# Attention feeding a swish MLP on one core: batches 0 and 1 piece by piece, and norms moved into early pass 2

## The chip, the cores and the metric

The kernel runs on one core of a Trainium2 chip. The metric is device time in microseconds (us), the median of several executions. A profile records one execution; its span is about 2 us shorter than the time of that execution (362.9 against 364.7 for the kernel before).

The engines are PE (matmuls and transposes; "PEld" is its weight load), DVE, ACT (exp, silu, copies), POOL, and SP, which issues DMAs. ACT and POOL can issue DMAs too. In the traces below each engine takes its own instructions in the order in which they were written: at 155.59 in the kernel before, a norm whose data had long been ready starts only when the evacuation written before it is done.

## The reference

```python
q_s = softmax(q, axis=-1)                 # over head_dim, 64
k_s = softmax(k, axis=2)                  # over the sequence, 576
kv  = einsum('bhsd,bhse->bhde', k_s, v)
out = einsum('bhsd,bhde->bhse', q_s, kv)  # batch 8, heads 8, seq 576, head_dim 64
x   = out.transpose(0, 2, 1, 3).reshape(4608, 512)
h   = x @ w_in                            # w_in 512 x 2048
g   = h / (1 + exp(-beta * h))
y   = g @ w_out                           # w_out 2048 x 512
```

## The kernel before

The 4,608 tokens form nine slabs: slabs 0 to 7 hold the first 512 tokens of batches 0 to 7, slab 8 the remaining 64 tokens of every batch. A slab has two passes of 64 matmuls of 128x512: pass 1 multiplies by w_in and applies silu (result in `GT`), pass 2 multiplies by w_out for four units `u` of 128 tokens, each of which is then evacuated: copied from PE's accumulators (`PS`) to `O2S`, from where it is stored. Attention of batch t+1 is spread as small steps between the matmuls of slab t; a counter of matmuls, the slot, says when a step is issued. Heads go in pairs, `hp` 0 to 3.

Attention of a batch consists of: exp of q and k (ACT), the norm of q (DVE: sum, reciprocal, multiply; `EQ`), the cast of v to bf16 (POOL; `VB` and the remainder `VR`), transposes of q (PE) and their copy to `QT`, the kv matmuls (PE), their masked and scaled copy `KVD` (DVE), the output matmul (PE), and the copy to `XT`, the input of pass 1.

```python
def norm_main(b, hp0, n):                      # three DVE instructions; a = EQ of n head pairs
    add(DVE, lambda e: e.tensor_reduce(s_, a, AX.X, ALU.add), ...)
    add(DVE, lambda e: e.reciprocal(v_, s_), ...)
    add(DVE, lambda e: e.tensor_tensor(a, a, vb, ALU.mult), ...)
def norm(b):
    norm_main(b, 0, 4)
    if b % 2 == 1:
        norm_rem()
# ... head: loads
add(ACTE, ... dma_start(BT, beta) ...)         # 8 KB, first on ACT's queue
load_main("qf", qt_h, QF, 0, split=4)          # SP
load_rem("krf", kt_h, KRF, 0, eng=ACTE)
load_main("kf", kt_h, KF, 0, eng=ACTE, split=4)
load_rem("vrf", vt_h, VRF, 0)
load_main("vf", vt_h, VF, 0, split=4)
gate = P.ops[-2]                               # the third of V's four loads
for c in range(8):                             # w_in, issued by POOL, cast to bf16 by the DMA
    add(POOL, lambda e, c=c, a=a: e.dma_start(WIN[:, :, 256 * c:256 * c + 256], a),
        ..., after=[gate] if c == 0 else ())
# ... head: batch 0
for hp in range(NHP):
    exp_main("q", QF, EQ, 0, hp, 1)
    norm_main(0, hp, 1)
exp_rem("k", KRF, EKR[0], ("ekr", 0))
cast_vr(0)                                     # POOL, behind the eight w_in issues
for hp in range(NHP):
    exp_main("k", KF, EK, 0, hp, 1)
    cast_v(0, hp)                              # POOL
    for s in t_steps(0, (hp,), HEAD) + kv_steps(0, (hp,), HEAD):
        s()
    if hp < 3:
        warm(3, 0)                             # matmuls on zeros
    for s in out_step(0, hp, HEAD, ACTE if hp % 2 else DVE):
        s()
# ... the slabs
for t in range(NSLAB):
    steps = attn(t + 1) if t < 7 else []
    lo, hi = {0: (90, 128), 1: (84, 128)}.get(t, (4, 112))   # slots of the steps
    ...                                        # pass 1; in slab 0 also the scaling of w_out
    if t == 0:
        prep(1)                                # exps and V casts
        norm(1)
    elif t == 1:
        prep(2)
        norm(2)
    for us in (((0, 1), (2, 3)) if t == 0 else ((0,), (1,), (2,), (3,))):
        pass2_group(t, us, tick)               # matmuls, then the evacuation to O2S (DVE)
        ...                                    # prep(3), or prep(t + 2) after unit 0
    if t == 1:
        norm(3)
    elif t >= 2 and t + 2 < B:
        norm(t + 2)                            # behind the last evacuation of the slab
    store(t)
```

The softmax here doesn't subtract the row's maximum and nothing guards it: scores larger than these inputs give would overflow.

## Time and profile before

| | before |
|---|---|
| median time | 366.3 us |
| span of the profile | 362.9 us |
| mean granted PE clock | 0.914 of full |
| PE busy | 299.7 us (83%) |

The first view is the profile's table of forty equal slices, 9.07 us each. A digit is the busy share in tenths; PEclk is the granted clock in tenths of full speed.

```profile
PE   5047973999569499959995999599959999999995
...
PEclk9559995799969899989999899889987999999999
```

From slice 14 on, the dips in the PE row come every four slices, at the starts of slabs 2 to 6; the earlier ones lie in the head and in pass 2 of slabs 0 and 1. PEclk dips with them or just after. The second view lists what PE waited for: total us, number of times, longest.

```profile
PE PS L340 <- DVE EQ L289: 38.0, 8, 7.2
PE PS L342 <- POOL VB L304: 13.9, 1, 13.9
```

The 38 us are waits of the transposes for the multiply of the norm. Of the eight waits one is in the head (2.9 us), one in slab 0 (6.7), one in slab 1 (7.2), and one at the start of each of slabs 2 to 6 (4.2 to 4.5 each). The 13.9 us is the head's wait for the first V cast, which stands on POOL behind the issues of w_in. In the lines of a timeline the columns are start, duration, engine (with a q where it only issues a DMA), line, operation, operands, count, and in brackets the idle time before it with its releaser:

```profile
14.65 6.16 POOL L473 DMA_DIRECT2D WIN<-in_moe_w_in_dram  x8 [9.27 <-DMA VF<-in_v_dram]
...
22.34 2.78 POOL L304 CAST VB<-VF 128x512 bf16<-128x512 f32 x4
```

The third view is the timeline at the start of slab 3, reduced to DVE and PE.

```profile
154.78 1.67 PE L342 MATMUL PS<-XT,WIN 128*128 128x512 bf16 x7
...
154.98 0.69 DVE L538 COPY O2S<-PS 128x512 f32<-128x512 f32 x1 [2.16 <-PE PS L342]
155.59 2.27 DVE L287 TENSOR_REDUCE QS<-EQ 128x32 f32<-128x2048 bf16 x1
...
158.28 2.29 DVE L289 TENSOR_TENSOR EQ<-EQ,QI 128x2048 bf16<-128x2048 bf16 x1
...
160.63 0.23 PE L340 MATMUL PS<-IDB,EQ 128*128 128x128 bf16 x1 [4.18 <-DVE EQ L289]
```

The norm's data were ready long before, but its instructions stand behind the last evacuation (154.98). PE does seven matmuls of the new slab, meets the first transpose, and waits.

The fourth view gives the busy time and clock by stage, with the stages cut at the first w_in matmul of a slab: the head, slab 0, slab 1, slab 2, slabs 3 to 6, slabs 7 and 8. Columns: stretch, its length, busy us and instructions of PE, PEld, DVE, ACT and POOL, the granted clock, the DMA share and GB/s.

```profile
0.00:32.60 32.60, 12.44 (x64) 6.15 (x66) 12.20 (x34) 6.77 (x11) 13.82 (x31) 0.74 1.00 209
32.60:77.10 44.50, 35.73 (x179) 16.47 (x181) 20.57 (x39) 20.19 (x29) 8.06 (x10) 0.85 0.99 303
77.10:116.90 39.80, 32.40 (x168) 15.30 (x170) 12.87 (x21) 23.02 (x36) 6.12 (x10) 0.91 0.66 200
116.90:154.80 37.90, 32.86 (x179) 15.68 (x181) 17.08 (x29) 18.35 (x27) 2.46 (x4) 0.95 0.40 126
154.80:303.70 148.90, 131.11 (x684) 63.07 (x697) 58.00 (x94) 66.06 (x97) 8.14 (x10) 0.93 0.16 54
303.70:362.90 59.20, 55.12 (x252) 24.92 (x255) 6.23 (x9) 22.01 (x32) 0.00 (x0) 0.99 0.15 54
```

In the last stage nothing but the passes is left, and 256 matmuls take 59.2 us with the tail; slab 7 alone takes 27.6. An estimate for a slab with attention is about 31 us: these 27.6 and some 3 us of attention matmuls (25 us for eight batches, by the sum in the prediction). A slab that takes longer is waiting or running at a lower clock.

### The profile page before, as it was taken

How to read it: one execution, taken by the hardware profiler on the slowest of the kernel's cores; microseconds unless marked ns; L12 is line 12 of the kernel's file. 1: busy time of each engine (PE TensorE's matmuls, PEld its weight loads, DVE VectorE, ACT ScalarE, POOL GpSimd, SP SyncE). 2: the span in 40 equal slices, each digit the busy share in tenths (PEclk: the TensorE clock that was granted, in tenths of full speed). 3: DMA queues.
4: the chain of work that ended last, by engine and by line, in shares of the span. 5: the costliest groups of instructions: out<-in, count | busy, mean ns of one | idle time of the engine just before them, and what ended most of it. 6: DMA issues, size and time to landing. Idle time of an engine off the chain costs nothing.

```text
span 362.9 us, 3757 instructions
## 1 busy us (share of the span) xinstructions
PE 299.7 (83%) x1514; PEld 141.6 (39%) x1544; DVE 127.0 (35%) x225; ACT 156.4 (43%) x232; POOL 38.6 (11%) x65
## 2 busy tenths in 40 slices
PE   5047973999569499959995999599959999999995
PEld 2023431544234155424442454244424544444442
DVE  3424418350255811560257125601571252011011
ACT  4105882038940178216822583158405603803710
POOL 4360004420004002030110020000000000000000
PEclk9559995799969899989999899889987999999999
DMA  8899899880399300960095000200020002002013
GB/s 225 212 162 264 315 316 337 235 274 36 121 313 337 127 2 11 342 169 0 5 321 167 0 2 0 116 3 0 3 116 0 0 2 116 2 0 116 2 29 87
DMA packets 45954, 44.29 MB, mean 122 GB/s; under 512 B 13665, under 2 KB 42353, under 8 KB 44913
## 3 DMA queue, kind: packets, MB, share of 16 engines
q1 hardware_dynamic: 39216, 40.11, 35.1%
q0 software_dynamic: 4224, 2.10, 4.6%
q10 hardware_dynamic: 2496, 1.84, 1.8%
q8 instruction: 12, 0.20, 0.2%
q14 instruction: 6, 0.04, 0.0%
HBM read 36.71 MB, written 9.44 MB: 127 GB/s over the span
## 4 chain that ended last, share of the span: by engine, by line
PE 68%; DVE 14%; DMA 11%; ACT 2%; SPq 2%; issue 1%; POOL 1%
PE PS L342 65%; DVE EQ L289 4%; DVE QS L287 4%; DMA QF<-in_q_dram 3%; PE PS L340 3%; DMA WIN<-in_moe_w_in_dram 3%; DMA VF<-in_v_dram 2%; DMA WST<-in_moe_w_out_dram 2%; DVE XT L406 1%; DVE O2S L538 1%; ACT EQ L273 1%; POOL WIN L473 1%; SPq L247 1%; DVE QI L288 1%; DVE KVD L390 1%
## 5 line engine op out<-in xcount | busy, mean ns | idle before, releaser
L533 ACT ACTIVATE GT<-PS,BETA 128x512 bf16<-128x512 f32 x144 | 98.8, 687 | 159.1 <-PE PS L342 158.8
L342 PE MATMUL PS<-WOUT,GT 128*128 128x512 bf16 x560 | 142.9, 388 | 2.0 <-DVE O2S L538 1.4
L342 PE MATMUL PS<-XT,WIN 128*128 128x512 bf16 x563 | 142.2, 397 | 1.1 <-DVE XT L406 0.4
L342 PEld LDWEIGHTS PS<-WOUT,GT 128*128 128x128 bf16 x576 | 52.8, 99 | 58.7 <-issue 3.6
L342 PEld LDWEIGHTS PS<-XT,WIN 128*128 128x128 bf16 x576 | 53.1, 102 | 57.5 <-issue 6.5
L340 PE MATMUL PS<-IDB,EQ 128*128 128x128 bf16 x128 | 29.4, 252 | 38.3 <-DVE EQ L289 38.0
L538 DVE COPY O2S<-PS 128x512 f32<-128x512 f32 x36 | 24.6, 688 | 75.6 <-PE PS L342 75.5
L342 PE MATMUL PS<-VB,EK 128*128 128x129 bf16 x128 | 26.2, 226 | 15.0 <-POOL VB L304 13.9
L340 PEld LDWEIGHTS PS<-IDB,EQ 128*128 128x128 bf16 x128 | 14.4, 116 | 55.8 <-DVE EQ L289 41.5
L304 POOL CAST VB<-VF 128x512 bf16<-128x512 f32 x32 | 21.5, 673 | 121.2 <-PE PS L342 89.1
L360 DVE COPY QT<-PS 128x1024 bf16<-128x1024 bf16 (+1 forms) x18 | 11.4, 631 | 55.4 <-PE PS L340 55.4
L287 DVE TENSOR_REDUCE QS<-EQ 128x32 f32<-128x2048 bf16 (+1 forms) x11 | 18.7, 1697 | 27.1 <-ACT EQ L273 27.1
L342 PEld LDWEIGHTS PS<-VB,EK 128*128 128x128 bf16 x128 | 12.3, 100 | 25.2 <-POOL VB L304 14.0
L388 DVE RECIPROCAL RC<-PS 128x1 f32<-128x1 f32 x32 | 5.2, 163 | 46.3 <-PE PS L342 46.3
L406 DVE CAST XT<-PS 128x512 bf16<-128x512 f32 x30 | 19.0, 684 | 2.0 <-PE PS L342 2.0
L289 DVE TENSOR_TENSOR EQ<-EQ,QI 128x2048 bf16<-128x2048 bf16 (+1 forms) x11 | 18.8, 1713 | 0.4
L273 ACT ACTIVATE EK<-KF 128x512 bf16<-128x512 f32 x32 | 17.7, 617 | 0.8 <-DMA KF<-in_k_dram 0.7
L273 ACT ACTIVATE EQ<-QF 128x512 bf16<-128x512 f32 x32 | 17.4, 614 | 0.8 <-DMA QF<-in_q_dram 0.8
L342 PE MATMUL PS<-QT,KVD 128*128 128x512 bf16 x32 | 12.6, 393 | 1.4 <-DVE KVD L390 1.3
L312 POOL CAST VR<-VRF 64x512 bf16<-64x512 f32 x8 | 6.9, 861 | 48.4 <-DMA VRF<-in_v_dram 47.8
L390 DVE SCALAR_TENSOR_TENSOR KVD<-PS,RC,MASK 128x128 bf16<-128x128 f32 x32 | 11.2, 351 | 1.1
L273 ACT ACT_TABLE_LOAD x7 | 9.0, 1283 | 5.2 <-issue 5.1
(41 smaller groups left out, 86.8 us busy)
## 6 DMA issues: line engine op xcount, KB each, us to landing
out_dram<-O2S SPq DMA_DIRECT2D x8, 1024.0 KB, 3.8
KF<-in_k_dram SPq DMA_DIRECT2D x7, 1024.0 KB, 6.3
QF<-in_q_dram SPq DMA_DIRECT2D x7, 1024.0 KB, 9.4
VF<-in_v_dram SPq DMA_DIRECT2D x7, 1024.0 KB, 11.1
WST<-in_moe_w_out_dram SPq DMA_DIRECT2D x4, 1024.0 KB, 5.8
WIN<-in_moe_w_in_dram POOLq DMA_DIRECT2D x8, 256.0 KB, 8.5
QF<-in_q_dram SPq DMA_DIRECT2D x4, 256.0 KB, 3.9
KF<-in_k_dram ACTq DMA_DIRECT2D x4, 256.0 KB, 7.1
```

The costliest lines, as they stand in the source:

```text
L273: add(ACTE, lambda e, o=o, a=a: e.activation(o, a, ACT.Exp), r=[(name + "f", i, hp)], w=[("e" + name, i, hp)])
L287: add(DVE, lambda e: e.tensor_reduce(s_, a, AX.X, ALU.add), r=ks, w=[("qs", i, hp0)])
L289: add(DVE, lambda e: e.tensor_tensor(a, a, vb, ALU.mult), r=ks + [("qi", i, hp0)], w=[("nq", i, hp) for hp in range(hp0, hp0 + n)] + ks)
L304: add(POOL, lambda e: e.tensor_copy(o, a), r=[("vf", i, hp), ("vone", i)], w=[("vb", i, hp)])
L312: add(POOL, lambda e, o=o, a=a: e.tensor_copy(o, a), r=[("vrf", h), ("vrone", pi, h), ("vr0", pi, h)], w=[("vr", pi, h)])
L340: add(PE, lambda e: e.transpose(o, l, r_), r=r, w=w, bank=[bk])
L342: add(PE, lambda e: e.matmul(o, l, r_, start=start, stop=stop), r=r, w=w, bank=[bk])
L360: add(DVE, lambda e: e.tensor_copy(o, pb[:, 0:w]), r=[("ps", st["b"])], w=[("qt", i, h) for h in hps], bank=[st["b"]])
L390: add(DVE, lambda e, t_=t_, h2=h2: e.scalar_tensor_tensor(KVD[i][:, h2, :], t_, RC[i][:, h2:h2 + 1], MASK[:, :], ALU.mult, ALU.mult), r=[( ...
L406: add(DVE, lambda e: e.tensor_copy(XT[i][:, hp, :], PS[bk][:, :]), r=[("ps", bk)], w=[("xt", i, hp)], bank=[bk])
L533: add(ACTE, lambda e: e.activation(GT[:, f, :], PS[bk][:, :], ACT.Silu, scale=BETA[:, f:f + 1]), r=[("ps", bk), "beta"], w=[("gt", f)], ba ...
L538: add(DVE, lambda e: e.tensor_copy(O2S[t % 2][:, u, :], PS[bk][:, :]), r=[("ps", bk)], w=[("o2", t % 2, u)], bank=[bk])
```

## The change

Its intent: start the first slab earlier by working on batch 0 as its pieces land and by taking the V casts off POOL; treat batch 1 in the same way between slabs 0 and 1; and issue each norm early enough that no transpose waits for it. The diff is shortened: `...` stands for what is cut, and the comments are added here. "Key sums" are the sums of exp(k), now matmuls of their own.

```diff
+        def attn_now(b, pool, wbank, wn, mid):            # batches 0 and 1
+            exp_q(b)
+            for hp in range(NHP):
+                norm_main(b, hp, 1, POOL if hp % 2 else DVE)   # odd pairs: multiply on POOL
+            mid()                                          # batch 0: issue w_in
+            ...                                            # transposes (copied by ACT), K exps,
+            ...                                            # key sums, V casts on ACT, warm matmuls
+            for hp in range(NHP):
+                bk = bank(pool)
+                ...                                        # five kv matmuls
+                kvd(b, hp, bk, 0)
+                warm(wn[4], wbank)
+                go(out_step(b, hp, pool))
-        add(ACTE, lambda e: e.dma_start(BT[:, :], ...beta...),
         load_main("qf", qt_h, QF, 0, split=4)
+        add(SP, lambda e: e.dma_start(BT[:, :], ...beta...),
-        load_rem("krf", kt_h, KRF, 0, eng=ACTE)
-        load_main("kf", kt_h, KF, 0, eng=ACTE, split=4)
+        load_rem("krf", kt_h, KRF, 0, (0,))                # now on SP
+        load_main("kf", kt_h, KF, 0, split=4)
 ...
-                w=[("win", c)], slot=f"win{c}", after=[gate] if c == 0 else ())
+                    w=[("win", c)], slot=f"win{c}", after=P.writer[("kf", 0, 3)] if c == 0 else ())
+                if c == 1:
+                    cast_vr(0, (0,))
 ...
+            if t == 1:
+                todo = spread([norm_rem] + tr_steps() + outr_steps(1), 16, 44)
+                todo += spread(attn_late(2), 86, 126)
+            elif 2 <= t < 7:
+                todo = spread(attn(t + 1), 28 if t == 2 else 8, 112)
+            if t == 2:
+                norm_main(3, 0, 4)
+                norm_rem()
 ...
+            if t == 0:                                     # w_out in three stages, not two
+                pass2_group(0, (0, 1, 2, 3), (3, 4, 5, 6), tick)   # four units at once
+                attn_now(1, (7, 0, 1, 2, 5, 6), 3, (0, 0, 6, 6, 1), lambda: cast_vr(1, (1,)))
 ...
+            for u in range(4):
+                pass2_group(t, (u,), (OB[orot[0] % 2],), tick)
+                if t >= 2 and nb:                          # nb = [t + 2]
+                    if u < 2:
+                        norm_main(nb[0], 2 * u, 2)
+                    elif u == 2 and nb[0] % 2:
+                        norm_rem()
-            elif t >= 2 and t + 2 < B:
-                norm(t + 2)
```

Also in it: ACT's first table load is pulled to the start by a tiny exp, and units 1 and 3 of slab 0 are evacuated by ACT.

## The prediction

It was written with the profile of the kernel before alone.

> **What bounds it now.** Span 362.9 us. By lines, the 1,152 matmuls of the MLP passes start every 0.216 us at full clock (249 us); attention adds about 25 us of PE work. The other 90 us is PE standing still or slow. By the timeline and PE's waits:
> - head: the first w_in matmul starts at 32.6. PE waits 13.9 us for the first V cast: POOL issues w_in (14.65 to 20.8), held until V has landed, before it casts.
> - slab 0 (32.6 to 77.1): w_out is scaled until 46.2, just before pass 2 (46.65); then 6.7 us wait for batch 1's norm, then half clock until 68.7.
> - slab 1 (to 116.9): 7.2 us wait for batch 2's norm, then half clock.
> - slabs 2 to 6 (186.8 us): each starts with 4.2 us waiting for the EQ multiply, as the 5 us norm is queued behind the previous slab's last evacuation; then about 1.5 us lost to half clock. A slab without that is about 31.1 us.
> - slabs 7, 8 and tail: 59.2 us, clean.
>
> The Trainium skill, "TensorE: Matmul & The Clock Gate", Part 1, has the mechanism: an idle window of about 3.4 us halves the clock. The trace agrees (0.43 us spacing after the 6.7 us wait).
>
> **What changes.**
> 1. Head: V casts move to ACT (0.6 us each), no longer behind w_in; w_in starts when K is in (about 10); V lands at 15 to 16.5; kv, KVD, output and XT after it cost about 3 us. Pass 1 starts at 19.5: **-13 us**. w_in and w_out finish about 3 us earlier, and pass 2 runs four units at once, needing a w_out piece only every 3.5 us. It ends at about 47.5.
> 2. Batch 1 is handled between slabs 0 and 1, not interleaved. Its exps stand behind two ACT evacuations and a table load (1.28); ACT needs about 10 us, then kv to XT: 14.5 us to the next pass 1. Slab 0 is about 42.5 us against 44.5: **-2 us**.
> 3. Slab 1: batch 2's norm comes in four pieces from slot 86, so the 7.2 us wait goes; but POOL does two multiplies (estimate 1.2 us: DVE's 0.69 and the ratio 1.96 in the skill, "GPSIMD Engine Reference", section 3.1) before its casts, so V casts come about 3 us late. About 36 against 39.8: **-4 us**.
> 4. Slabs 2 to 6: norms of batches 4 to 7 run in early pass 2; batch 3's is covered by starting at slot 28. The five waits and half clocks go (31 us with transitions), but 3 us norm blocks on DVE delay KVD and XT late in pass 2, about 1.2 us in slabs 2 to 5: 161 us: **-26 us**.
> 5. Slabs 7, 8: the same.
>
> All of it lies on the PE chain, so it counts in full: -45 to -47.
>
> **Prediction.** Span about 316; the median is 2 to 3 us over the span: **318 us**, range 307 to 331. Chances: faster by over 2% 0.97, within 2% 0.02, slower 0.01.
>
> **What would show it.** First w_in matmul near 19.5; slab 1's first near 62, slab 2's near 98; no PE wait on EQ in slabs 3 to 6, granted clock near 1.0 there, slabs of 31 to 32.5 us; 12 to 15 us between slabs 0 and 1, ACT the busiest; V casts of batch 2 holding PE in slab 1's pass 2.
>
> **What would make it wrong.** w_in and V sharing the DMA engines so V lands after 18 or w_in starves pass 1; w_out late for pass 2; batch 1's stretch over 17 us; DVE norms blocking pass 2 by over 3 us a slab. If norms hide fully and batch 1 takes 11 us, 308.

## The result

| | before | after |
|---|---|---|
| median time | 366.3 us (364.9 to 366.7, 4 runs) | 327.6 us (327.0 to 328.9, 4 runs) |
| span | 362.9 us | 325.4 us |
| mean granted clock | 0.914 | 0.983 |
| PE busy | 299.7 us (83%) | 293.5 us (90%) |

The ratio is 0.895 (95% interval 0.892 to 0.899). Ratios here are the mean time of one kernel's runs over that of the other's of the same rounds, so they are not quite the ratio of the medians quoted.

The same four views of the kernel after. The slices are 8.1 us each.

```profile
PE   4769992879949999999989989999899999999995
...
PEclk9999998799989999999999999999999999999999
```

The regular dips are gone; behind the head two remain, at slice 7 (between slabs 0 and 1) and slice 12 (pass 2 of slab 1). PE's waits:

```profile
PE PS L345 <- DVE KVD L380: 7.9, 11, 1.5
PE PS L343 <- DVE EQ L308: 6.8, 2, 4.4
PE PS L345 <- POOL VB L323: 3.5, 1, 3.5
PE PS L343 <- DMA BT<-in_moe_beta_dram: 2.8, 1, 2.8
```

The two EQ waits left are in the head (2.5) and between slabs 0 and 1 (4.4). The stages, cut in the same way:

```profile
0.00:22.40 22.40, 13.26 (x83) 6.07 (x85) 9.77 (x27) 12.42 (x21) 12.78 (x28) 1.00 0.86 192
22.40:68.90 46.50, 37.62 (x201) 17.51 (x204) 16.84 (x37) 24.79 (x39) 2.69 (x3) 0.93 1.11 296
68.90:106.90 38.00, 33.48 (x178) 15.63 (x181) 14.63 (x32) 23.02 (x36) 9.78 (x15) 0.96 0.75 212
106.90:138.50 31.60, 31.22 (x178) 15.12 (x180) 21.46 (x34) 18.36 (x27) 5.23 (x8) 1.00 0.74 221
138.50:266.20 127.70, 122.83 (x684) 60.40 (x697) 53.58 (x100) 66.05 (x97) 6.15 (x10) 1.00 0.18 63
266.20:325.40 59.20, 55.12 (x252) 24.92 (x255) 6.22 (x9) 21.99 (x32) 0.00 (x0) 0.99 0.15 54
```

The head's clock of 1.00 in this table is not a measurement: the clock record of this trace begins only at 13.8 us, and what comes before counts as full. Matmuls on zeros before that start 0.43 us apart, which is half clock. In the kernel before, the record begins at 3.9, so the mean clocks (0.914 and 0.983) are not quite alike.

At the start of slab 3, where PE waited 4.18 us before the change, the first transpose now comes without a wait:

```profile
138.54 1.89 PE L345 MATMUL PS<-XT,WIN 128*128 128x512 bf16 x7
140.27 0.22 PE L343 MATMUL PS<-IDB,EQ 128*128 128x128 bf16 x1
```

Subtracting the two tables gives the bill of the change, set beside the predicted terms. The predicted term for slabs 2 to 6 was a single one.

| stage | before | after | difference | predicted |
|---|---|---|---|---|
| head | 32.6 | 22.4 | -10.2 | -13 |
| slab 0 | 44.5 | 46.5 | +2.0 | -2 |
| slab 1 | 39.8 | 38.0 | -1.8 | -4 |
| slabs 2 to 6 | 186.8 | 159.3 | -27.5 | -26 |
| slabs 7, 8, tail | 59.2 | 59.2 | 0 | 0 |
| span | 362.9 | 325.4 | -37.5 | -45 |

So nearly three quarters come from slabs 2 to 6, where the norms moved and the steps of batch 3 start later. The stages that got the most new code, the head and slab 0, gave 8 us where 15 were expected.

The head, first, in the timeline. DVE's four beta operations come before the norms in its order:

```profile
2.76 0.46 SPq L533 DMA_DIRECT2D BT<-in_moe_beta_dram  x1
...
3.64 1.30 ACT L280 ACTIVATE EQ<-QF 128x512 bf16<-128x512 f32 x2 [1.40 <-DMA QF<-in_q_dram]
...
7.91 0.17 DVE L559 TENSOR_SCALAR BC<-PS 128x16 f32<-128x16 f32 x1 [5.99 <-PE PS L343]
...
8.70 0.63 DVE L306 TENSOR_REDUCE QS<-EQ 128x8 f32<-128x512 bf16 x1
...
13.85 1.04 POOL L308 TENSOR_TENSOR EQ<-EQ,QI 128x512 bf16<-128x512 bf16 x1 [1.52 <-DVE QI L307]
...
14.83 1.73 POOL L573 DMA_DIRECT2D WIN<-in_moe_w_in_dram  x2
```

The first exp of q ends near 4.3 us, but its sum starts at 8.70: DVE is idle for 6 us before the beta operations, and from 4.3 on it is the beta vector alone that it waits for, 8 KB that landed at about 7.5; its load now stands behind the q loads on SP. And w_in is issued at 14.83, not at about 10: POOL does the second multiply of the norm first. It was 14.65 before the change, so "w_in once K is in" did not happen at all. The late norms delay V as well, on ACT: there the copies of q's transposes stand before the last K exps and the V casts. V's four loads landed from 12.65 to 14.74, but the first cast started at 15.77.

Between slabs 0 and 1 (pass 2 ends at 50.5, slab 1 starts at 68.9), ACT's order decides:

```profile
50.15 1.07 ACT L604 COPY O2S<-PS 128x512 f32<-128x512 f32 x2 [12.69 <-PE PS L345]
...
51.24 1.28 ACT L280 ACT_TABLE_LOAD   x1
...
52.54 2.19 ACT L280 ACTIVATE EQ<-QF 128x512 bf16<-128x512 f32 x4
...
54.91 0.61 PE L343 MATMUL PS<-IDB,EQ 128*128 128x128 bf16 x4 [4.36 <-DVE EQ L308]
```

Later in that stretch each head pair runs kv matmuls, KVD, output matmul strictly one after another; from one output matmul to the next is 1.43 us (64.37, 65.81, 67.24, 68.67).

### The profile page after: what moved, and what is told of

It reads as the page before. It is cut to its first block, busy times and chain, and to the rows that moved or that the text cites. A ratio compares the mean times of both kernels' runs of the same rounds, so it can differ in the third digit from the quotient of the medians.

```text
span 325.4 us, 3908 instructions
## 1 busy us (share of the span) xinstructions
PE 293.5 (90%) x1569; PEld 139.6 (43%) x1600; DVE 122.5 (38%) x238; ACT 166.6 (51%) x252; POOL 36.6 (11%) x63
## 4 chain that ended last, share of the span: by engine, by line
PE 78%; DVE 13%; ACT 2%; POOL 2%; issue 2%; DMA 1%; SPq 1%; POOLq 0%; DVEq 0%
PE PS L345 76%; DVE QS L306 3%; DVE EQ L308 3%; DVE XT L417 2%; PE PS L343 2%; DVE KVD L380 2%; DMA BT<-in_moe_beta_dram 1%; DVE O2S L604 1%; DVE QI L307 1%; POOL EQ L308 1%; ACT L280 1%; POOL VR L331 1%; SPq L251 1%; ACT EQ L280 0%; ACT O2S L604 0%
## 5 line engine op out<-in xcount | busy, mean ns | idle before, releaser
L345 PE MATMUL PS<-WOUT,GT 128*128 128x512 bf16 x564 | 136.9, 382 | 0.5
L345 PE MATMUL PS<-XT,WIN 128*128 128x512 bf16 x560 | 132.5, 379 | 1.1
L343 PE MATMUL PS<-IDB,EQ 128*128 128x128 bf16 x128 | 25.2, 233 | 9.0 <-DVE EQ L308 6.8
L345 PE MATMUL PS<-VB,EK 128*128 128x129 bf16 (+2 forms) x160 | 26.6, 212 | 4.7 <-POOL VB L323 3.5
L363 DVE COPY QT<-PS 128x1024 bf16<-128x1024 bf16 x12 | 8.3, 690 | 40.2 <-PE PS L343 40.2
L306 DVE TENSOR_REDUCE QS<-EQ 128x8 f32<-128x512 bf16 (+2 forms) x21 | 19.9, 947 | 8.7 <-ACT EQ L280 8.7
L323 POOL CAST VB<-VF 128x512 bf16<-128x512 f32 x24 | 15.4, 642 | 63.8 <-PE PS L345 62.8
L343 PEld LDWEIGHTS PS<-IDB,EQ 128*128 128x128 bf16 x128 | 11.8, 103 | 20.2 <-DVE EQ L308 7.9
L308 DVE TENSOR_TENSOR EQ<-EQ,QI 128x1024 bf16<-128x1024 bf16 (+2 forms) x15 | 16.8, 1119 | 0.5
L345 PE MATMUL PS<-WARM 128*128 128x512 bf16 x37 | 14.5, 508 | 1.3 <-DVE WARM L219 1.2
L308 POOL TENSOR_TENSOR EQ<-EQ,QI 128x512 bf16<-128x512 bf16 x6 | 6.3, 1042 | 73.7 <-DVE QI L307 73.7
```

What stands on the lines that cost most here:

```text
L306: add(DVE, lambda e: e.tensor_reduce(s_, a, AX.X, ALU.add), r=ks, w=[("qs", i, hp0)])
L308: add(eng, lambda e: e.tensor_tensor(a, a, vb, ALU.mult), r=ks + [("qi", i, hp0)], w=ks)
L323: add(eng, lambda e: (e.copy if eng == ACTE else e.tensor_copy)(o, a), r=[("vf", i, hp), ("vone", i)], w=[("vb", i, hp)])
L343: add(PE, lambda e: e.transpose(o, l, r_), r=r, w=w, bank=[bk])
L345: add(PE, lambda e: e.matmul(o, l, r_, start=start, stop=stop), r=r, w=w, bank=[bk])
L363: add(eng, lambda e: (e.copy if eng == ACTE else e.tensor_copy)(o, pb[:, 0:w]), r=[("ps", st["b"])], w=[("qt", i, h) for h in hps], bank=[ ...
```

## The experiments

The stages of each run are read as above, from the first w_in matmul of each slab. "Gain" is against the changed kernel's 327.6 us unless said otherwise. Runs came on different chips, each beside runs of the kernel before; the changed kernel was not run again beside them. The medians of the kernel before were 364.4 to 364.7 there and 366.3 beside the changed kernel, so a gain in us may be off by up to 1.9, and small differences are judged by the stage that was edited.

### a_norm_late: only the norms of batches 4 to 7 back at the end of the slab

```diff
-                if t >= 2 and nb:
-                    if u < 2:
-                        norm_main(nb[0], 2 * u, 2)
-                    elif u == 2 and nb[0] % 2:
-                        norm_rem()
             while todo:
                 todo.pop()[1]()
+            if t >= 2 and nb:
+                norm_main(nb[0], 0, 4)
+                if nb[0] % 2:
+                    norm_rem()
```

> The changed kernel with one part undone: the norms of batches 4 to 7 stand behind the last evacuation of each slab again. Theory 1 (where the norms run is what removed the waits of slabs 3 to 6): PE again waits on the EQ multiply once in each of slabs 3 to 6, 3 to 4 us each, while the KVD waits of 1.2 to 1.5 us late in pass 2 of slabs 2 to 5 go; net 11 to 20 us longer than the changed kernel, 339 to 348 us. Theory 2 (the later start and the new spacing of the attention steps removed them): within 3 us of 327.6.

Measured: 349.6 us, ratio 0.959 (0.953 to 0.964). Slabs 3 to 6 took 151.2 us at clock 0.91 in place of 127.7 at 1.00; the other stages kept their length within 0.9 us. Its waits:

```profile
PE PS L343 <- DVE EQ L308: 23.3, 6, 4.4
PE PS L345 <- DVE KVD L380: 3.8, 8, 0.6
```

Four EQ waits came back (23.3 - 6.8 = 16.5 us, 4.1 each), and KVD waits fell from 7.9 to 3.8. The theory of where the norms stand holds. The time came out 1.6 us above the expected range, because each wait costs more than itself: four waits of 4.1 us made the four slabs 23.5 us longer, the rest being half clock, for 6.8 us at each wait. That is net of the 4.1 us of KVD waits that went.

### b_norm_only: the kernel before, with only the norms moved

```diff
                 pass2_group(t, us, tick)
+                if t >= 2 and t + 2 < B:
+                    if us[-1] in (1, 2):
+                        norm_main(t + 2, 2 * us[-1] - 2, 2)
+                    elif us[-1] == 3 and t % 2:
+                        norm_rem()
 ...
-            elif t >= 2 and t + 2 < B:
-                norm(t + 2)
```

> The kernel before with this one part added: the norms of batches 4 to 7 in pass 2 behind the evacuations of units 1 and 2. Theory 1: four of the five 4.2 us waits and their half clocks go, at most 1.5 us each comes back as KVD waits: 366.3 less 16 to 24 us, 342 to 350 us, head and slabs 0 and 1 unchanged. Theory 2 (the waits need the later step start): less than 8 us gained.

Measured: 340.0 us, ratio 0.933 (0.928 to 0.938); the runs of the kernel before beside it had a median of 364.6, so the gain is 24.6 us. Slabs 3 to 6 took 124.8 us in place of 148.9. The five lines moved give more than half of the whole change's 38.7 us, without any of the new code. The value lies below the expected 342 to 350 for the same reason as in the run before. (In its profile two stages that were not edited differ too: slab 0 took 3.0 us less and slab 2 1.6 us more.) The step start left at slot 4 did no harm.

### c_bt_first: the beta load first, on ACT's queue

```diff
+        add(ACTE, lambda e: e.dma_start(BT[:, :], ...beta...), w=["bt"], slot="bt")
         load_main("qf", qt_h, QF, 0, split=4)
-        add(SP, lambda e: e.dma_start(BT[:, :], ...beta...), w=["bt"], slot="bt")
```

> The changed kernel with the 8 KB beta load issued first, from ACT, as in the kernel before. Theory 1 (in the changed kernel beta lands at 7.6 us behind q, and the four beta operations stand ahead of the norms on DVE, which holds the first norm from 4.4 to 8.7 us and with it the whole head): first w_in matmul at 18.8 to 20 in place of 22.45, time 2 to 4 us less than 327.6. Theory 2 (the head is bound by when K and V land): first w_in matmul at 22 to 22.5, time unchanged within 1 us.

Measured: 325.6 us, ratio 0.894 (0.890 to 0.898). The load landed 2.5 us after its issue instead of 4.8; the first norm sum started at 5.78, w_in was issued at 11.91, and the first w_in matmul came at 20.2 instead of 22.4. The head gained 2.2 us, slightly less than expected, and the span fell by the same 2.2. The theory holds; the interval of the ratio alone would not show it, the stage does.

### d_kv_pipe: the output matmul one head pair later

```diff
                 warm(wn[4], wbank)
-                go(out_step(b, hp, pool))
+                if hp:
+                    go(out_step(b, hp - 1, pool))
+            go(out_step(b, NHP - 1, pool))
```

> The changed kernel with the output matmul of a head pair issued after the next pair's kv matmuls, in both stretches done piece by piece. Theory 1 (PE waits out each KVD in turn, 1.43 us a pair): each of the two stretches 1.2 to 1.8 us shorter; 2.5 to 3.5 us less than 327.6. Theory 2 (the stretches are bound by the V casts on ACT): under 1 us.

Measured: 324.7 us, ratio 0.890 (0.887 to 0.894). The first w_in matmul came at 20.5 (2.0 us earlier). The stretch between slabs 0 and 1 went from 18.4 to 17.3 us, a little less than expected. Together these are 3.1 of the 3.4 us by which the span fell. The serial chain of KVD cost this; V casts did not set it.

### e_norm2_dve: batch 2's multiplies all on DVE

```diff
                     for hp in range(NHP):
-                        norm_main(2, hp, 1, POOL if hp % 2 else DVE)
+                        norm_main(2, hp, 1)
```

> The changed kernel with all four norm multiplies of batch 2 on DVE. Theory 1 (two multiplies of 1.04 us on POOL stand before the V casts and make them late): the 3.5 us wait on the V cast in pass 2 of slab 1 falls to under 1 us and the half clock after it goes; slab 1 33.5 to 35 us in place of 38.0; 3 to 4.5 us less than 327.6. Theory 2 (the casts are late because their data or buffers are): the wait stays above 2.5 us.

In the changed kernel, the timeline of POOL and the PE matmul that it holds:

```profile
89.17 1.04 POOL L308 TENSOR_TENSOR EQ<-EQ,QI 128x512 bf16<-128x512 bf16 x1 [29.05 <-DVE QI L307]
91.74 1.04 POOL L308 TENSOR_TENSOR EQ<-EQ,QI 128x512 bf16<-128x512 bf16 x1 [1.52 <-DVE QI L307]
92.91 1.35 POOL L331 CAST VR<-VRF 64x512 bf16<-64x512 f32 x2
...
95.06 0.23 PE L345 MATMUL PS<-VB,EK 128*128 128x129 bf16 x1 [3.53 <-POOL VB L323]
```

POOL does not reach the V casts until 94.4, because it waits for DVE's reciprocals before each of its two multiplies. Measured with the edit: 323.8 us, ratio 0.889 (0.886 to 0.893); slab 1 took 34.3 us in place of 38.0, at clock 1.00 in place of 0.96. The V cast wait is gone; in its place stands one of 1.9 us for an evacuation on DVE, which is now queued behind the norm. The theory holds.

### f_win_after_v: w_in held until V has landed

```diff
-                    ..., after=P.writer[("kf", 0, 3)] if c == 0 else ())
+                    ..., after=P.writer[("vf", 0, 3)] if c == 0 else ())
```

> The changed kernel with w_in held until V has landed, as before the change. In the changed kernel w_in was issued from 14.83, held by the second multiply on POOL and not by K. Theory 1 (the earlier gate is worth little: V lands near 14.5 and pass 1 never waits for w_in): within 1 us of 327.6, first w_in matmul 22 to 23. Theory 2 (the gate on K is what starts w_in early enough): pass 1 of slab 0 waits for w_in, 2 to 5 us more.

Measured: 329.2 us, ratio 0.902 (0.899 to 0.906). w_in was issued at 14.61 and the first w_in matmul came at 22.2, the same as without the edit: the gate is not what starts w_in there. The median is 1.6 us higher, outside the 1 us expected. The profile puts that into stages that the edit does not touch: the stretch between slabs 0 and 1 took 19.5 us in place of 18.4, with the same 4.4 us wait in it, and slab 1 39.0 us at clock 0.91 in place of 38.0 at 0.96, with the same 3.5 us wait. Run h, which leaves slab 1 alone as well, has 38.7 us at 0.91. How much half clock follows a wait differs from run to run; "The clock" below shows on what it hangs.

### l_bt_first_win_v: the last run, both edits together

This is c_bt_first with the gate of f_win_after_v, to see the gate where nothing else holds w_in.

> The run with beta first (325.6 us, w_in issued from 11.9, first w_in matmul at 20.2) with w_in held until V has landed. Theory 1 (the gate on K is worth something once nothing else holds w_in): w_in is issued from 13 to 14.5, and either pass 1 of slab 0 starts later or waits for w_in, or w_out comes late for pass 2; pass 2 of slab 0 starts more than 1 us later than 34.3. Theory 2 (w_in has slack in any case): pass 2 starts within 0.5 us of 34.3 and the time is within 1.5 us of 325.6.

Measured: 329.7 us, ratio 0.903 (0.898 to 0.907). Now the gate binds: w_in is issued at 14.81, and the first w_in matmul comes at 22.9 instead of 20.2, pass 2 of slab 0 at 37.0 instead of 34.3. But PE waits for something else than w_in:

```profile
14.81 1.74 POOL L573 DMA_DIRECT2D WIN<-in_moe_w_in_dram  x2 [2.78 <-DMA VF<-in_v_dram]
16.54 0.63 POOL L331 CAST VR<-VRF 64x512 bf16<-64x512 f32 x1
...
17.22 0.29 PE L345 MATMUL PS<-VR,EKR 128*128 128x128 bf16 x1 [2.60 <-POOL VR L331]
```

The cast of V's remainder stands behind the first two w_in issues in POOL's order. In pass 1 no wait for w_in appears. So the gate on K is worth 2.7 us once beta is early, through POOL's order and not because w_in was late. In the changed kernel as it stands it is worth nothing. (The span of this run's profile is 5.0 us longer than c's; the other 2.3 us are more half clock after the same two waits, as in run f.)

### g_no_warm1: no warming matmuls in batch 1's stretch

```diff
-                attn_now(1, (7, 0, 1, 2, 5, 6), 3, (0, 0, 6, 6, 1), ...)
+                attn_now(1, (7, 0, 1, 2, 5, 6), 3, (0, 0, 0, 0, 0), ...)
```

> The changed kernel without the 16 warming matmuls in batch 1's stretch. Theory 1 (at half clock they hold up the transposes and key sums behind them): the stretch from the last pass-2 matmul of slab 0 to the first w_in matmul of slab 1 1 to 2.5 us shorter than 18.35, but slab 1 starts at half clock[...], so the total is within 1.5 us of 327.6. Theory 2 (they earn their place): slower by more than 1.5 us, with half clock in pass 1 of slab 1.

Measured: 327.3 us, ratio 0.898 (0.894 to 0.901). The stretch fell by 1.3 us to 17.1, and pass 1 of slab 1 grew from 14.8 to 16.1 us, at clock 0.90 in place of 1.00. The two cancel: the warming matmuls neither cost nor earn anything in this position.

### h_norm_u2: the second half of the norms behind unit 2

```diff
                 if t >= 2 and nb:
-                    if u < 2:
-                        norm_main(nb[0], 2 * u, 2)
-                    elif u == 2 and nb[0] % 2:
+                    if u % 2 == 0:
+                        norm_main(nb[0], u, 2)
+                    elif u == 3 and nb[0] % 2:
                         norm_rem()
```

> The changed kernel with the second half of each norm (batches 4 to 7) moved from behind unit 1 to behind unit 2, when the attention steps are done. Theory 1 (the second 3 us norm block delays KVD and XT): the KVD waits of 1.2 to 1.5 us in slabs 2 to 5 go, 3 to 5 us less than 327.6. Theory 2 (the wait comes back as one on EQ at the start of the next slab, or the first block is as costly): unchanged within 1 us.

What was to be removed, in pass 2 of slab 3 of the changed kernel:

```profile
161.98 1.21 DVE L306 TENSOR_REDUCE QS<-EQ 128x16 f32<-128x1024 bf16 x1
...
163.51 1.23 DVE L308 TENSOR_TENSOR EQ<-EQ,QI 128x1024 bf16<-128x1024 bf16 x1
165.72 0.39 PE L345 MATMUL PS<-QT,KVD 128*128 128x512 bf16 x1 [1.46 <-DVE KVD L380]
```

Measured: 325.4 us, ratio 0.893 (0.889 to 0.896). Half right. Slabs 3 and 5 fell from 32.2 to 30.5 us each; slabs 2 and 4 stayed at 31.7 and 32.3, and the longest KVD wait was still 1.2 us. Slab 4 handles an odd batch, which has more steps, so its last kv matmuls come earlier, while the first norm block is running (190.04 to 192.80 here, with the reciprocal for KVD at 192.72). Slab 2 handles an odd batch too, but its steps start at slot 28, and it had no KVD wait to lose, in the changed kernel either. The gain in the edited stages is 3.3 us; slab 1, not edited, was 0.7 us longer in this run (38.7 against 38.0, see f).

### i_q1_early: batch 1's q ahead of the evacuations

```diff
+        def attn_pre(b):
+            exp_q(b)
+            for hp in range(NHP):
+                norm_main(b, hp, 1, POOL if hp % 2 else DVE)
 ...                                            # attn_now calls it for batch 0 only
+                attn_pre(1)
                 pass2_group(0, (0, 1, 2, 3), (3, 4, 5, 6), tick)
```

> The changed kernel with batch 1's q exps and norms issued before pass 2 of slab 0 instead of behind its evacuations; q has landed by 47, pass 2 ends at 50.5. Theory 1 (the stretch between slabs 0 and 1 is long because the exps stand behind the evacuations and the table load on ACT, so PE waits 4.4 us for the first norm): that wait goes, the stretch is 13 to 15 us in place of 18.35, 3.5 to 5.5 us less than 327.6. Theory 2 (the chain after the norms, K exps, V casts and the kv matmuls, sets its length): the stretch stays above 16.5 us, under 2 us gained.

Measured: 324.8 us, ratio 0.891 (0.888 to 0.894). The stretch is 14.7 us (50.1 to 64.8) in place of 18.4, as the first theory has it; the 4.4 us wait is gone. The time fell by only 2.8 us, below the expected 3.5, because slab 1 took 38.9 us: the same 3.5 us V cast wait was followed by more half clock (0.86 over pass 2, against 0.93).

### j_all and k_all_k1_early: the gains together

Run j combines c, d, e and i, and puts the norm halves behind units 1 and 2 in even slabs and 0 and 2 in odd ones, as run h suggested.

> Together: beta first on ACT, output matmuls one pair later, batch 2's multiplies on DVE, batch 1's q early, and the norm halves of batches 4 to 7 behind units 1 and 2 in even slabs, 0 and 2 in odd ones. If each gain adds (2.2, 3.4, 3.4, 4, and 1.5 for each of slabs 2 to 5), the time is 310 to 315 us; if the head and the stretch have a common next limit (w_out landing before pass 2 of slab 0, K and V landing), 315 to 319. KVD waits of over 1 us gone from slabs 2 to 5.

Measured: 311.3 us, ratio 0.854 (0.851 to 0.857): the gains add, and no KVD wait is longer than 0.5 us. Run k moves batch 1's K exps ahead of the evacuations too.

```diff
+            if b == 1:
+                exp_kr(b, (1,))
+                exp_k(b)                        # in attn_pre; attn_now does them for batch 0 only
```

> The run before this one, with batch 1's K exps also ahead of the evacuations of slab 0. Theory 1 (ACT's queue still sets the stretch): 2 to 3 us less than that run. Theory 2 (K lands only at about 50, so the evacuations now wait behind the exps, or the V casts set the length): within 1 us of it.

Measured: 308.1 us, ratio 0.845 (0.841 to 0.849), 3.2 us less than j: ACT's order still set the stretch, which went from 14.0 to 11.0 us. Its stages, cut as before up to slab 1:

```profile
0.00:17.70 17.70, 13.42 (x85) 6.58 (x86) 9.41 (x27) 12.41 (x21) 11.76 (x27) 1.00 0.95 222
17.70:56.80 39.10, 35.32 (x205) 16.76 (x203) 16.75 (x39) 25.20 (x39) 3.67 (x5) 1.00 1.15 297
56.80:92.60 35.80, 33.56 (x181) 15.73 (x182) 15.87 (x34) 23.02 (x36) 7.87 (x12) 0.95 1.04 283
```

Slab 1 took 35.8 us at clock 0.95 here and 34.2 at 1.00 in j, with the same PE wait of 2.0 us for an evacuation in both; why is told under "The clock".

Kernel k gives the right result and beats both kernels: 19.5 us less than the changed one, 56 us less than the kernel before by the medians of its own rounds (308.1 against 364.4).

## Why the prediction was right or wrong

**The total was close, and its error has an address.** 318 us was predicted, 327.6 measured. The gain was forecast at 45 to 47 us of span; it was 37.5. The missing 7.5 us are in the first three stages (head, slab 0, slab 1: -19 predicted, -10.0 measured). The later slabs came out 1.5 us better than predicted, which hid some of it. One of the prediction's own conditions for being wrong was met: batch 1's stretch took 18.4 us, over its 17.

**Slabs 2 to 6: right, mechanism and size.** The waits on EQ are gone, the clock there is 1.00, and slabs take 31.0 to 32.3 us (predicted 31 to 32.5). The forecast side effect, KVD waits "about 1.2 us in slabs 2 to 5", is there in slabs 3, 4 and 5 (1.5, 1.2 and 1.5 us) and not in slab 2. Run a undoes this part and loses 22 us, run b does it alone and gains 24.6. Run h shows that the side effect depends on which batch is handled, which the prediction lumped together.

**Head: right about moving the V casts, wrong about what then holds them; off by 2.8 us.** Predicted: first w_in matmul at 19.5. Measured: 22.4. Two terms failed.
- "w_in starts when K is in (about 10)". It started at 14.83. The prediction read the dependency and not what stands in front of it: in POOL's order the second norm multiply comes first, and that one hung on the beta vector, whose load the change put behind q. The diff showed the load's move and the prediction passed over it. The late w_in by itself cost little: its first piece landed at 18.72 and PE never waited for it; only the cast of V's remainder, behind the first two issues on POOL, held PE for 0.4 us. What delayed the first w_in matmul were the norms, and behind them on ACT the V casts, although V landed earlier than the predicted 15 to 16.5 (12.65 to 14.74). Run c, with beta early, recovers 2.2 us.
- "kv, KVD, output and XT after it cost about 3 us". That counted the last pair only. Four pairs run one after another at 1.43 us each, so the last output matmul comes 5.8 us after the first pair's kv matmuls (16.43 to 22.22). Run d recovers 2.0 us.

With both mended, run j starts at 18.5, 3.9 us earlier. That is more than the 2.9 by which 19.5 was missed, so other terms of the sum were a little too high.

**Slab 0: wrong by 4 us.** Predicted 42.5 us, measured 46.5. The passes themselves were right (36.6 for the start of pass 2 less 22.4, and 50.5 for its end: 28.1 us, predicted 28). The term that failed is "14.5 us to the next pass 1": it was 18.4. The reason named, exps behind evacuations and the table load, is right, since run i removes it and gets 14.7. Missing from the sum were the serial pairs again (1.1 us by run d), the warming matmuls, which hold up the transposes behind them (1.3 us by run g, given back as half clock), and POOL's multiplies on the way to the transposes (a wait of 1.35 us at 56.87, which no run removed by itself). That run i comes so near to the predicted 14.5 is chance: the prediction had counted the delay that this run takes away.

**Slab 1: mechanism right, size off by 2.2 us.** "V casts come about 3 us late": 3.5 measured, and run e confirms the cause. The prediction did not charge the clock for it: the mean clock of slab 1 is 0.96, and without the wait it is 1.00 (run e).

**The clock.** The prediction took the mechanism from the Trainium skill, "TensorE: Matmul & The Clock Gate", Part 1, which also says that the activity windows are free-running. The runs agree. In the clock records of all 14 packed traces every change lies on one grid per trace, with steps of 3.41 us (95.72 and 99.14 in the changed kernel). Summing PE's idle time in each of the 1,292 windows of these grids gives a rule for these traces: a window at full clock was followed by one at half clock when PE had been idle for about 2.0 of its 3.41 us or more (44 windows, 1.99 to 3.41), and was not when it had been idle for less (1,155 windows, up to 2.00). The clock came back after a window at half clock with at most 0.65 us of idle time (44 windows), and not with 0.77 or more (49).

So what a wait costs hangs on how it lies on the grid. The 2.0 us wait of slab 1 is the plainest case; in the columns of the stages, first k, then j:

```profile
78.31:81.72 3.41, 1.42 (x11) 0.72 (x10) 3.34 (x6) 3.41 (x8) 3.12 (x4) 1.00 1.02 314
81.72:85.13 3.41, 3.41 (x15) 1.56 (x12) 0.91 (x3) 2.57 (x4) 0.10 (x1) 0.50 1.08 361
...
83.51:86.92 3.41, 1.66 (x13) 0.96 (x14) 2.82 (x6) 3.39 (x8) 0.00 (x0) 1.00 0.96 333
86.92:90.33 3.41, 3.41 (x27) 1.94 (x26) 1.72 (x6) 1.20 (x1) 0.00 (x0) 1.00 1.11 346
```

In k the whole wait falls into one window, and half clock follows; in j a part of it (83.27 to 83.51) falls into the window before, and none does. In the same way the 3.5 us wait for the V cast left one window of half clock in the changed kernel and in runs c, d and g, and two in a, f, h, i and l. In f it was cut in two (2.2 us idle in one window, 1.4 in the next), so the second did not bring the clock back. The executions of one kernel may differ for this reason as well (the four of the changed kernel took 327.0 to 328.9 us), but only one of these has its trace here, so that is not shown.

**What stays open.** Of the head's gain, no run tests by itself that moving the V casts from POOL to ACT removed the 13.9 us wait; the trace shows the wait gone and w_in issued no earlier than before. The gain in slab 2 (6.3 us, by the later start of batch 3's steps) and the four units at once in slab 0 were not tested by themselves either. The two waits that kernel k still has on evacuations in the stretch between slabs 0 and 1, 1.7 and 1.2 us, were not tried, nor was the EQ wait of 2.5 us in its head.

## What to carry to other kernels

An instruction starts when its data are there and its queue has reached it. For each early start that a change promises, read what stands before that instruction on its own engine; here a small beta load, a multiply and two evacuations held up everything behind them. Price a wait of PE at more than its length where it can idle PE for over 2 us of one clock window (four waits of 4.1 us cost 23.5 us here, and one of 2.0 us was followed by 3.4 us of half clock in run k and by none in run j). And look for the few lines that remove repeated waits before rewriting a stage: five lines gave 24.6 of 38.7 us.

## What the Trainium skill lacked or had wrong

- "ScalarE: Activation LUTs", section "What ACT_TABLE_LOAD costs", gives 1283 ns for the load and about 1380 ns of drain for every switch. The load agrees (1.28 us), but no drain shows here: in the changed kernel the copies end at 51.22, the load runs from 51.24 to 52.52, and the first exp starts at 52.54. Copies go before the load there, and exps after it; at the load for silu in the same stretch an exp ends at 64.39 and the load starts at 64.41.
- "GPSIMD Engine Reference", section 3.1, gives the ratio 1.96 to DVE for a two-input operation, at 2048 elements of fp32. At 128x512 bf16 the multiply took 1.04 us on POOL and 0.69 on DVE, a ratio of 1.5. (The prediction's estimate of 1.2 us is not the product of its two figures: 0.69 times 1.96 is 1.35.) What the multiply cost here was not its length but its place ahead of the casts, about which the page says nothing.
- "DMA: Bandwidth & Descriptors", section "Issuing engines are not separate DMA queues", says that issuing from several engines only saves issue time, usually small. For the 8 KB of beta the time from issue to landing fell as well: 4.8 us behind four q loads on SP, 2.5 us when ACT issued it first (run c), worth 2.2 us of the span. Run c changed the engine and the place in the order together, so which of the two did it is not shown.
- "TensorE: Matmul & The Clock Gate", Part 1, has the clock halved after an idle window of about 3.4 us, and gives no share of idle time at which a partly idle window counts. In these traces 2.0 us of idle time within one window was enough (run k, 1.99 us), and 0.77 us in a window at half clock kept it there.
